# Fixed instruction orders, weight loads spread over the first segment, and a first K projection by halves, in a fused attention and gated-MLP kernel

## The chip, the cores and the metric

The kernel runs on one core of one Trainium2 chip. Times are device microseconds (us) of that core: medians over the executions listed with each result. One core has no second die to compare with, so a run counts as disturbed only if it is over 1.5% above the fastest of the same kernel. TensorE is called PE below, VectorE DVE, ScalarE ACT, GpSimd POOL and SyncE SP.

## The reference

Two branches read the same 2048 x 512 input and are mixed by a gate for each token. The attention branch has 32 heads of 16, four segments of 512 tokens, causal softmax inside a segment, and a linear memory carried from one segment to the next.

```python
for s in range(4):                                  # segments of 512 tokens
    logits = einsum('bhqd,bhkd->bhqk', qs, ks) * scale + mask   # causal
    p = softmax(logits); a_dot = einsum('bhqk,bhkd->bhqd', p, vs)
    num = einsum('bhld,bhde->bhle', phi(qs), M)     # memory of earlier segments
    den = einsum('bhld,bhd->bhl', phi(qs), z)[..., None] + 1e-06
    o = g * (num / den) + (1.0 - g) * a_dot         # g = sigmoid(beta), per head
    M = M + einsum('bhld,bhle->bhde', phi(ks), vs); z = z + phi(ks).sum(l)
a = concat(o) @ wo
b = (gelu(x @ w_gate) * (x @ w_up)) @ w_down        # 512 -> 1792 -> 512
gt = sigmoid((x * gate_w).sum(-1))
return gt * a + (1 - gt) * b
```

## The kernel before

The program is a graph of about a thousand tasks. A list scheduler runs while the kernel is built: it takes, over and over, the task that can start first by its own model of durations, with a priority (longest path plus a tuned bias for each kind of task) to break ties. The order in which it takes tasks becomes the fixed order of instructions on each engine. Each engine counts its finished instructions in one semaphore, so whoever waits for a task waits until the engine has passed that place in its list.

```python
while len(order) < n:
    for e in ENGINES:
        for t in ready[e]:
            st = max(cur[e], ready_at[t.id])
            ...                                   # exp first on ACT, patience for PV
            k = (st, -t.prio - (OPEN_BONUS if open_ else 0.0), t.id)
            if best is None or k < best[0]: best = (k, e, t)
```

The tasks that matter here, all for one segment s and a group t of eight heads: `qk` (row-tiled matmuls, 32 rows each, into one 2048-column PSUM tile), `exp` (ACT), `msk` (POOL zeroes what causality forbids), `pv` (column-tiled matmuls), `pvt` and `norm` (DVE). A task name such as `exp1_1B0` means segment 1, group 1, part B0; part L is the low rows. `G`, `U`, `D` are the gate, up and down matmuls, `K`, `Q`, `V` the projections, and a name with `ev` is the copy of its result out of PSUM. The masks and the loads before the change:

```python
# low rows: one select over 2048 columns
masks = [(PTl[:].rearrange("p g (b c) -> p (g b) c", c=64), [[0, 32], [2, 64]], 1, 2048)]
# other parts: one select of 256 columns for each key block
(bass.AP(PT[slot], c, [[2048, P], [512, 4], [1, 64]]), [[0, 4], [1, 64]], 64, 256) for c in offs
...
for a in range(4):
    dma(f"x0_{a}", (SP, ACT)[a % 2], ...)                     # x of segment 0
for c0, c1 in ((0, 128), (128, 512)):                         # columns 0-127, then the rest
    for key, w, src in (("wk", wk, A_wk), ("wq", wq, A_wq)):
        wdma((key, c0 > 0), SP, w[:, :, c0:c1], ...)
wdma("wv", ...); ...; wdma(("wg", 0), ...); wdma(("wg", 1), ...)
...
# after the first transposes of segment 0, in one lump on one queue
wdma(("wu", 0), ..., after=pk0); wdma(("wu", 1), ..., after=pk0)
wdma("wd", ..., after=pk0); wdma("wo", ..., after=pk0)
```

The softmax here doesn't subtract the row's maximum and nothing guards it: scores larger than these inputs give would overflow.

Of the kernel before, what the change touches and what calls it, by code (L numbers as in the profile page):

```python
# [13 lines left out]
ALU = mybir.AluOpType  # L14
# [18 lines left out]
PV_JOIN = 0.11  # L33
HOLD = 0.3
OPEN_BONUS = 6.0
BIAS = {
    "D0": -705, "D1": -805, "D2": -380, "D3": -442, "G0": -222, "G1": -900, "G2": -744, "G3": -86, "GdT0": 97,
    "GdT1": 844, "GdT2": -1, "GdT3": 895, "Gev0": 862, "Gev1": -349, "K0": 777, "K1": -529, "K2": 250,
    "K3": 307, "Q0": 715, "Q1": -519, "Q2": 584, "Q3": -641, "U0": -844, "U1": -888, "U2": -53, "U3": -206,
    "Um0": 900, "Um1": 148, "Um2": 49, "Um3": -86, "V0": 318, "V1": -357, "V3": 539, "Vev0": 540, "Vev1": 758,  # L40
    "Vev2": 262, "Vev3": -72, "Vlo0": -900, "Vlo1": 900, "Vlo2": -70, "Vlo3": 237, "consts": 21, "exp0": -666,
    "exp1": 177, "exp2": -517, "exp3": -395, "exsT0": 77, "exsT1": -899, "exsT2": -94, "exsT3": 695, "fin0": 37,
    "fin1": -471, "fin2": 741, "fin3": -517, "gbd": -146, "gelu0": -795, "gelu1": 416, "gelu2": 1, "gelu3": 126,
    "gexp": 402, "gexs0": -594, "gexs1": -701, "gexs3": 76, "gmat": -900, "gmul1": 900, "gmul2": -10,
    "gmul3": 319, "gsum0": -318, "gsum1": -86, "gsum2": -613, "gsum3": -900, "gts0": 73, "gts1": -850,
    "gts2": -487, "gts3": 848, "ident": 503, "kl0": -826, "kl1": -900, "kl2": -661, "kl3": 900, "kp0": 509,
    "kp1": 3, "kp2": -900, "kp3": -405, "masks": 769, "msk0": -290, "msk1": 789, "msk2": 116, "msk3": -63,
    "mz0": -162, "mz1": 638, "mz2": -319, "mzacc0": -423, "mzacc1": 170, "mzacc2": 439, "mzbd0": -25,
    "mzbd1": -178, "mzbd2": 70, "norm0": 704, "norm1": -880, "norm2": -46, "norm3": 166, "num2": -887,
    "num3": -200, "nump1": -900, "nump2": -220, "nump3": -164, "oTd1": 896, "oTd2": 268, "oTd3": 899,  # L50
    "omg": 528, "out0": 408, "out1": -644, "out10": 2, "out11": 869, "out12": 745, "out13": 461, "out14": -25,
    "out15": -280, "out2": 230, "out3": -27, "out4": 313, "out5": -134, "out6": 284, "out7": -18, "out8": 682,
    "out9": -139, "pkT0": 5, "pkT1": 569, "pkT2": 281, "pkc0": 489, "pkc1": -900, "pkc2": -14, "pke0": 310,
    "pke1": 399, "pke2": -73, "pqc1": 496, "pqc2": 14, "pqc3": -117, "pqe1": -17, "pqe2": 649, "pqe3": 63,
    "pv0": -95, "pv1": -551, "pv2": -900, "pv3": 30, "pvt0": -169, "pvt1": 86, "pvt2": -513, "pvt3": -26,
    "qk0": 417, "qk1": 185, "qk2": 503, "qk3": 669, "tload": 355, "vones": -877, "w": -765, "warm0": 21,
    "warm1": 747, "warm2": -324, "warm3": 371, "warm4": 223, "warm5": -120, "warm6": -334, "x0": -96,
    "x0ev0": 93, "x0ev1": 23, "x0t0": 596, "x0t1": 606, "x1": 367, "x2": -181, "x3": -900, "xt1": 533,
    "xt2": -189, "xt3": 11
# [42 lines left out]
class Task:  # L102


    def __init__(self, name, alts, grp=None, after=(), bias=0.0, nbytes=0):
        self.name = name
        self.alts = alts
        self.grp = grp
        self.after = tuple(after)
        self.bias = bias + BIAS.get(name[:re.search(r"[_.]|$", name).start()], 0.0)  # L110
        self.nbytes = nbytes
        self.tiled = None
        self.patience = 0.0
        self.ahead = False
        self.est = {e: sum(i.est for i in l) for e, l in alts.items()}
        rs, ws = set(), set()
        for l in alts.values():
            for i in l:
                rs.update(i.reads)
                ws.update(i.writes)  # L120
        self.reads, self.writes = rs, ws
        self.preds, self.succs = set(), set()
        self.prio = 0.0
        self.eng = None
        self.start = self.finish = None
        self.id = None


class Sched:
# [32 lines left out]
    def schedule(self):  # L162
        tasks = self.tasks
        n = len(tasks)
        groups = defaultdict(list)
        for t in tasks:
            if t.grp is not None:
                groups[t.grp].append(t)
        for g in groups.values():
            for t in g[1:]:  # L170
                for d in () if t.ahead or PE in t.alts else t.preds:
                    if d.grp is not g[0].grp and d not in g[0].preds:
                        g[0].preds.add(d)
                        d.succs.add(g[0])
        indeg = [len(t.preds) for t in tasks]
        topo = [t for t in tasks if indeg[t.id] == 0]
        for t in topo:
            for s in t.succs:
                indeg[s.id] -= 1
                if indeg[s.id] == 0:  # L180
                    topo.append(s)
        assert len(topo) == n, "cycle"
        for t in reversed(topo):
            best = max([s.prio for s in t.succs] + [0.0])
            t.prio = min(t.est.values()) + best + t.bias
        npred = [len(t.preds) for t in tasks]
        ready_at = [0.0] * n
        ready = {e: set() for e in ENGINES}
        for t in tasks:
            if npred[t.id] == 0:  # L190
                for e in t.alts:
                    ready[e].add(t)
        cur = {e: 0.8 for e in ENGINES}
        bank_free = {b: 0.0 for b in range(self.nbanks)}
        dma_free = 0.0
        order = []
        last_pe = None
        while len(order) < n:
            best = None
            due = min([ready_at[t.id] for t in ready[ACT] if t.tiled == "exp"] + [1e9])  # L200
            held = sum(t.tiled == "pv" and ready_at[t.id] <= cur[PE] + HOLD for t in ready[PE])
            for e in ENGINES:
                for t in ready[e]:
                    st = max(cur[e], ready_at[t.id])
                    if e == ACT and t.tiled != "exp" and st + t.est[e] > due + 0.1:
                        continue
                    if t.tiled == "pv":
                        if last_pe in ("qk", "pv") and ready_at[t.id] <= cur[e] and bank_free and \
                                min(bank_free.values()) <= cur[e]:
                            if best is None or (-1.0, 0.0, t.id) < best[0]:  # L210
                                best = ((-1.0, 0.0, t.id), e, t)
                            continue
                        st += t.patience
                    if t.grp is not None and t.grp.bank is None:
                        if len(bank_free) <= (0 if t.tiled == "pv" else held):
                            continue
                        st = max(st, min(bank_free.values()))
                    open_ = t.grp is not None and t.grp.bank is not None
                    k = (st, -t.prio - (OPEN_BONUS if open_ else 0.0), t.id)
                    if best is None or k < best[0]:  # L220
                        best = (k, e, t)
            assert best is not None, "deadlock in task graph"
            (st, _, _), e, t = best
            if t.tiled == "pv":
                st = max(cur[e], ready_at[t.id], min(bank_free.values()))
            for a in t.alts:
                ready[a].discard(t)
# [5 lines left out]
            if e == PE:  # L233
                if t.tiled == "pv" and last_pe == "pv":
                    t.finish -= PV_JOIN
                last_pe = t.tiled
# [14 lines left out]
            for s in t.succs:  # L251
# [3 lines left out]
                if npred[s.id] == 0:  # L255
                    for a in s.alts:
                        ready[a].add(s)
# [116 lines left out]
def _build(es, nc, A_x, A_wq, A_wk, A_wv, A_wo, A_beta, B_w_gate, B_w_up, B_w_down, gate_w, out):  # L374
# [108 lines left out]
    rank = [9000.0]  # L483
# [5 lines left out]
    def wdma(key, eng, dst, src, nbytes, nonc=False, after=()):  # L489
        rank[0] -= 20.0  # L490
        dma("w_" + str(key), eng, lambda: dst, lambda: src, [], [("w", key)], nbytes, bias=rank[0], nonc=nonc,
            after=after)

    def xdma(s, after=()):
        for kb in range(4):
            rank[0] -= 20.0
# [14 lines left out]
              [("c", "ident")], [("c", "ident")], 0.3)], bias=9990.0)  # L511
    task("tload", ACT, [Instr(lambda e: e.activation(stmp[:, 0:1], ones[:, 0:1], ACTF.Exp), writes=[("stmp",)],
                              est=1.5)], bias=8000.0)
    xin = hT[1][:, 0:4, :]
    for a in range(4):
        rank[0] -= 20.0
        dma(f"x0_{a}", (SP, ACT)[a % 2], lambda a=a: xin[:, a, :], lambda a=a: A_x[0, a * 128:(a + 1) * 128, :], [],
            [("hT", 1, a)], 131072, bias=rank[0], issue=0.45)
    for c0, c1 in ((0, 128), (128, 512)):
        for key, w, src in (("wk", wk, A_wk), ("wq", wq, A_wq)):  # L520
            wdma((key, c0 > 0), SP, w[:, :, c0:c1], r4(src)[:, :, c0:c1], 1024 * (c1 - c0) * (2 if c0 == 0 else 1))
    wdma("wv", SP, wv[:], r4(A_wv), 524288)
# [606 lines left out]
```

## Time and profile before

| | kernel before |
|---|---|
| time | 269.44 us, median of 3 (269.11 to 269.78) |
| span of the profiled run | 267.5 us |
| PE busy | 96%, full granted clock in every slice |
| chain of waits | 84% PE, 5% ACT, 1% POOL |
| first Q matmul / last matmul starts | 9.84 us / 264.58 us |

From the page of the kernel before: the span, the busy time of each engine, PE's granted clock in 40 slices (tenths), and the shares of the chain that ended last.

```profile
span 267.5 us, 7093 instructions
...
PE 257.9 (96%) x2965; PEld 118.4 (44%) x3005; DVE 199.9 (75%) x385; ACT 212.1 (79%) x188; POOL 102.3 (38%) x232
...
PEclk9999999999999999999999999999999999999999
...
PE 84%; ACT 5%; DVE 3%; issue 3%; DMA 2%; POOL 1%; SPq 0%; ACTq 0%; DVEq 0%
...
```

PE is the bound, and it has almost no room. A busy PE is not yet a PE at its peak, so I use the starts of consecutive matmuls in the trace and take off their columns at 2.4 per ns. Columns are 236.1 us of the span (the four tiles of a QK or PV group run side by side, so each counts for a quarter of its columns). What is left over is 27.8 us: about 3 ns for each plain matmul, 19 us of fixed gaps at 167 mode changes (whole array, row tiles, column tiles, with the memory update counted apart from PV: the gap is 0.11 or 0.15 us after QK, by the columns of its last matmul, 0.12 after PV, 0.10 after plain matmuls), 3.3 us in the head (the cold clock and the wait for wk), and about 1.8 us of real stalls, that is, of gaps beyond the usual one at their place. The Trainium skill, "TensorEngine Tiling (Array Packing)", Key Properties, says that changing the tiling mode drains TensorE; the gaps agree with it. "TensorE: Matmul & The Clock Gate", section "Wait — 56ns, not 53.3ns?", gives columns / 2.4 GHz plus about 2.5 ns for a warm matmul; this trace has 2.7 (median).

The table of waits of the kernel before: engine, line and tile, what was waited for: total us, times, longest.

```profile
...
POOL pt L814 <- ACT pt L810: 126.6, 55, 16.9
...
PEld psXALL L803 <- ACT pt L810: 22.5, 52, 0.7
...
POOL ptl L814 <- ACT ptl L810: 9.0, 5, 2.0
...
```

POOL waits for ACT's exps in 55 waits of 2.3 us on average: it follows them one by one, and for the low-row mask (`ptl`) it waits 9.0 us in all. PE's weight loads wait for exps, but that is hidden. The timeline of PE in the head of the kernel before (start us, duration us, engine, line, operation, tiles, count, idle before and releaser):

```profile
...
3.67 1.91 PE L540 MATMUL psXALL<-ident,hT 128*128 128x128 bf16 x16
5.45 1.50 PE L449 MATMUL psW<-xT,wk 128*128 128x256 bf16 x8
7.24 2.76 PE L449 MATMUL psW<-xT,wk 128*128 128x512 bf16 x12 [0.28 <-DMA wk<-in_A_wk_dram]
9.84 1.46 PE L449 MATMUL psW<-xT,wq 128*128 128x512 bf16 x6
```

All of x is transposed first, then K starts with the first 128 columns of wk, waits 0.28 us (0.45 between starts) for the others, and Q follows at 9.84 us.

### The profile page before, as it was taken

To read this page: it belongs to the slowest core of one execution; us is meant where nothing else is said; L and a number is where in the kernel's file an instruction comes from. 1 tells how busy PE (TensorE), PEld (TensorE's weight loads), DVE (VectorE), ACT (ScalarE), POOL (GpSimd) and SP (SyncE) were. 2 spreads that over 40 slices of the span, in tenths; PEclk is the share of its full clock that TensorE was granted. 3 is DMA by queue.
4 is the path that set the end of the run, shared out by engine and by line. 5 is a ranking of instruction groups with operands and counts; after the bars stand their busy time and mean duration, and the time that the engine had idled before them with its cause. 6 is when DMAs were issued, how large, how long until landed. Compare 5 with 4: busy or idle time off the path is not lost.

```text
span 267.5 us, 7093 instructions
## 1 busy us (share of the span) xinstructions
PE 257.9 (96%) x2965; PEld 118.4 (44%) x3005; DVE 199.9 (75%) x385; ACT 212.1 (79%) x188; POOL 102.3 (38%) x232
## 2 busy tenths in 40 slices
PE   8999999999999999999999999999999999999996
PEld 5444444344443443434354444444344444444354
DVE  1769799898989898889756877987952688753451
ACT  4889988899998997998858998887767767777602
POOL 8364553873002433485201433486300252352300
PEclk9999999999999999999999999999999999999999
DMA  6998992000203443000021224010020025001002
GB/s 192 228 328 184 390 241 42 1 2 0 44 0 79 81 101 102 22 20 2 0 44 39 42 59 124 21 44 2 0 44 0 2 59 42 0 22 36 8 0 78
DMA packets 33775, 18.22 MB, mean 68 GB/s; under 512 B 21456, under 2 KB 33744, under 8 KB 33744
## 3 DMA queue, kind: packets, MB, share of 16 engines
q1 hardware_dynamic: 33456, 17.51, 27.0%
q8 instruction: 23, 0.38, 0.6%
q10 hardware_dynamic: 288, 0.26, 0.3%
q14 instruction: 8, 0.07, 0.1%
HBM read 9.84 MB, written 2.10 MB: 45 GB/s over the span
## 4 chain that ended last, share of the span: by engine, by line
PE 84%; ACT 5%; DVE 3%; issue 3%; DMA 2%; POOL 1%; SPq 0%; ACTq 0%; DVEq 0%
PE psW L449 68%; PE psXALL L803 8%; PE psW L852 5%; ACT pt L810 3%; DMA wk<-in_A_wk_dram 2%; PE psXALL L449 1%; PE psW L860 1%; POOL exsT L712 1%; DVE tb L867 0%; PE psW L769 0%; ACT L937 0%; ACT L926 0%; SPq L480 0%; DVE mzbd L784 0%; DVE phkt L692 0%
## 5 line engine op out<-in xcount | busy, mean ns | idle before, releaser
L810 ACT ACTIVATE pt<-psXALL 128x2048 bf16<-128x2048 f32 x64 | 120.1, 1876 | 26.0 <-PE psXALL L803 23.9
L814 POOL TENSOR_SCALAR_AFFINE_SELECT pt<-pt 128x256 bf16<-128x256 bf16 x128 | 59.2, 464 | 131.6 <-ACT pt L810 126.6
L449 PE MATMUL psW<-xT,wu 128*128 128x512 bf16 x216 | 51.9, 380 | 0.8 <-issue 0.6
L449 PE MATMUL psW<-xT,wg 128*128 128x512 bf16 x214 | 50.2, 380 | 1.7 <-issue 1.3
L449 PE MATMUL psW<-wd,hT 128*128 128x512 bf16 x203 | 50.3, 380 | 0.9 <-issue 0.8
L958 DVE TENSOR_TENSOR hT<-psW,hT 128x512 bf16<-128x512 f32 x56 | 37.5, 684 | 11.4 <-PE psW L449 10.9
L449 PEld LDWEIGHTS psW<-xT,wg 128*128 128x128 bf16 x224 | 20.4, 98 | 25.7 <-issue 2.5
L449 PEld LDWEIGHTS psW<-xT,wu 128*128 128x128 bf16 x224 | 20.4, 98 | 24.5 <-issue 2.3
L867 DVE STREAM_TRANSPOSE tb<-psW 128x512 f32<-128x512 f32 x32 | 21.3, 697 | 12.6 <-PE psW L860 12.2
L449 PEld LDWEIGHTS psW<-wd,hT 128*128 128x128 bf16 x210 | 18.8, 98 | 22.5 <-issue 2.5
L803 PE MATMUL psXALL<-qT,kpad 32*128 32x320 bf16 (+3 forms) x512 | 25.8, 273 | 0.3 <-ACT pt L810 0.3
L937 ACT ACTIVATE hT<-psW 128x512 bf16<-128x512 f32 x28 | 15.9, 601 | 7.0 <-PE psW L449 6.9
L814 POOL TENSOR_SCALAR_AFFINE_SELECT ptl<-ptl 128x2048 bf16<-128x2048 bf16 x8 | 16.9, 2117 | 9.4 <-ACT ptl L810 9.0
L803 PEld LDWEIGHTS psXALL<-qT,kpad 32*128 32x128 bf16 x512 | 7.7, 92 | 27.6 <-ACT pt L810 19.6
L852 PE MATMUL psW<-pt,vaug 128*17 128x192 bf16 (+3 forms) x512 | 18.7, 273 | 0.0
L810 ACT ACTIVATE ptl<-psXALL 128x2048 bf16<-128x2048 f32 x8 | 15.0, 1876 | 3.6 <-PE psXALL L803 3.6
L449 PE MATMUL psW<-xT,wk 128*128 128x512 bf16 (+1 forms) x64 | 16.1, 376 | 0.8 <-issue 0.5
L712 POOL COPY exsT<-exs 32x4 f32<-32x4 f32 x64 | 15.4, 241 | 3.7
L466 DVE CAST hT<-psW 128x512 bf16<-128x512 f32 x21 | 14.1, 683 | 2.8 <-PE psW L449 2.5
L449 PE MATMUL psW<-wo,oT 128*128 128x512 bf16 x55 | 15.2, 380 | 0.5 <-issue 0.3
L449 PE MATMUL psW<-xT,wq 128*128 128x512 bf16 x60 | 14.9, 380 | 0.7 <-ACT qT L463 0.4
L449 PE MATMUL psW<-wv,xT 128*128 128x512 bf16 x62 | 15.0, 380 | 0.3 <-issue 0.3
(98 smaller groups left out, 300.0 us busy)
## 6 DMA issues: line engine op xcount, KB each, us to landing
out_dram<-ost SPq DMA_DIRECT2D x15, 128.0 KB, 1.7
wg<-in_B_w_gate_dram SPq DMA_DIRECT2D x2, 896.0 KB, 6.1
wu<-in_B_w_up_dram SPq DMA_DIRECT2D x2, 896.0 KB, 5.9
wd<-in_B_w_down_dram SPq DMA_DIRECT2D x1, 1792.0 KB, 12.1
phkt<-in_A_x_dram SPq DMA_DIRECT2D x3, 512.0 KB, 4.1
vlow<-vaug SPq DMA_DIRECT2D x8, 136.0 KB, 2.9
wv<-in_A_wv_dram SPq DMA_DIRECT2D x1, 512.0 KB, 6.2
wo<-in_A_wo_dram SPq DMA_DIRECT2D x1, 512.0 KB, 9.7
```

The source lines that it names most:

```text
L449: return Instr(lambda e: e.matmul(view(), lhsT, rhs, start=first, stop=last), reads=reads, writes=[fkey if fkey is not None else g.key], e ...
L466: alts[DVE] = [Instr(lambda e: e.tensor_copy(dst(), src()), reads=reads, writes=writes, est=dve_t(n))]
L712: cross = task(f"exsT{s}", POOL, [Instr(lambda e, g=g, c=c: e.tensor_copy(exsT[sl][32 * g:32 * g + 32, c:16:4], exs[32 * c:32 * c + 32, s4 ...
L803: instrs.append(Instr(lambda e, g=g, lhs=lhs, rhs=rhs, c0=c0, ncol=ncol: e.matmul(X[g][:, c0:c0 + ncol], lhs(32 * g), rhs(32 * g), start=T ...
L810: prev_exp[0] = exp_task(s, f"exp{s}_{t}{name}", [Instr(lambda e: e.activation(dst[:], XALL[:, :].rearrange("p (g c) -> p g c", g=4), ACTF ...
L814: task(f"msk{s}_{t}{name}", POOL, [Instr(lambda e, view=view, pat=pat, base=base: e.affine_select(out=view, in_=view, compare_op=ALU.is_ge ...
L852: instrs.append(Instr(lambda e, t=t, q=q, kb=kb, slot=slot, c0=c0: e.matmul(gp.f32()[32 * q:32 * q + 17, 128 * kb + 64:512], Vaug[sl][:, k ...
L860: instrs.append(Instr(lambda e, t=t, q=q, kb=kb, c0=c0: e.matmul(gp.f32()[32 * q:32 * q + 17, 128 * kb:128 * kb + 64], Vlow[j][:, kb, 4 * ...
L867: task(f"pvt{s}_{t}_{j}", DVE, [Instr(lambda e: e.transpose(Tb[:, j, :], gp.f32()[:, :]), [gp.key], [("Tb", j)], dve_t(512))], grp=gp)
L937: lambda e, g=g, ft=ft, s=s: e.activation(hT[s % 2][:, ft, :], g.f32()[:, :], ACTF.Gelu_apprx_tanh),
L958: task(f"Um{s}_{ft}", DVE, [Instr(lambda e, g=g, ft=ft: e.tensor_tensor(hT[sl][:, ft, :], g.f32()[:, :], hT[sl][:, ft, :], ALU.mult), [g.k ...
```

## The change

The scheduler no longer searches: every engine gets a list of task names and takes them in that order. The order is given as data (the lists are long and cut here); the model's durations were refined, among them a term for PE's mode switches, one for its cold start and one for blocks of 256 instructions. The low-row mask becomes four selects of 512. The first wk arrives as four groups of full rows ahead of the second half of x, and the first K projection runs by halves of the tokens and by weight rows. wu, wd (now in two halves) and wo wait for named exps of segment 0 instead of going out together. Also in the change, and not cut out below: wq and wv come by halves of their rows, the first Q projection goes to the PSUM tile of QK (`psXALL`), x of later segments is loaded at other places, and some copies move between ACT and DVE. The intent seems to be to fix an order found elsewhere, to keep PE fed at the start, and to keep big loads out of the way of small ones.

```diff
-BIAS = { "D0": -705, "D1": -805, ... }
+SWITCH = 0.097
+COLD = 5.8
+BLOCK, BLOCK_ASK, BLOCK_END = 256, 165, 208
+ORDER = {
+    "pe": ( "warm6 warm1 ... x0t0_0 x0t1_0 K0_2.0 K0_0.0 ... x0t0_1 x0t1_1 K0_2.2 ... Q0_0.0 ..." ),
+    "act": ( ... ),
+    "dve": ( "... mzbd0 gmul1 K1_3ev GdT0 Gev1_2 pvt0_0_1 ... mzbd2 Vev3_0 norm2_1 K3_2ev K3_0ev kp3_1 ..." ),
+    "pool": ( "... msk0_0B0 msk0_0L msk0_0A0 msk0_0B1 gbd msk0_0A1 omg exsT0 ..."
+              " msk1_0A1 msk1_1B1 msk1_1B0 msk1_1A1 msk1_1A0 msk1_2A0 ..." ),
+    "sp": ( ... ),
+}
 ... (schedule)
-                for t in ready[e]:
-                    ...
-                    k = (st, -t.prio - (OPEN_BONUS if open_ else 0.0), t.id)
+                t = queue[e][-1]
+                if npred[t.id]:
+                    continue
 ... (head)
-    for c0, c1 in ((0, 128), (128, 512)):
-        for key, w, src in (("wk", wk, A_wk), ("wq", wq, A_wq)):
-            wdma((key, c0 > 0), SP, w[:, :, c0:c1], r4(src)[:, :, c0:c1], ...)
+    x0dma(0)
+    x0dma(1)
+    for kb in range(4):
+        wdma(("wk", kb), (SP, ACT)[kb % 2], wk[:, kb, :], A_wk[128 * kb:128 * kb + 128, :], ...)
+    x0dma(2)
+    x0dma(3)
 ... (K projection)
-        nu = 2 if even is not None else 1
+        nu = 2 if head and wkey == "wk" else 1
 ... (low-row mask)
-                masks = [(PTl[:].rearrange("p g (b c) -> p (g b) c", c=64), [[0, 32], [2, 64]], 1, 2048)]
+                masks = [(PTl[:, g, :].rearrange("p (b c) -> p b c", c=64), [[0, 8], [2, 64]], 1, 512)
+                         for g in range(4)]
 ... (big weights)
-    wdma(("wu", 0), ..., after=pk0)
-    wdma(("wu", 1), ..., after=pk0)
-    wdma("wd", ..., after=pk0)
-    wdma("wo", ..., after=pk0)
+    for i, e in enumerate(("exp0_0B1", "exp0_1B0")):
+        wdma(("wu", i), ..., after=pk0 + [at[e]])
+    for i, e in enumerate(("exp0_2A0", "exp0_3A0")):
+        wdma(("wd", i), ..., after=[at[e]])
+    wdma("wo", ..., after=[at["exp0_3A1"]])
```

## The prediction

> **What bounds the kernel now.** TensorE, from the first weights to the end. The page gives PE 96% busy, full granted clock in every slice, and the chain of waits is 84% PE. A busy PE is not a PE at its peak, so I set the starts of consecutive matmuls in the trace against their columns. Between 7.24 us (K projection after its last wait) and the last matmul's start at 264.6 us nearly everything is accounted for:
> - about 233 us of columns at 2.4 per ns, plus about 3 ns per matmul, 3 us;
> - 167 changes between whole-array, row-tiled (QK) and column-tiled (PV) matmuls, each a fixed gap: 0.15 us after QK, 0.10 after plain matmuls, 0.13 after PV, about 21 us in all. The Trainium skill, "TensorEngine Tiling (Array Packing)", Key Properties, says that a mode change drains TensorE; these gaps agree;
> - other stalls: only about 0.6 us (0.3 at 100 us, 0.2 at 85 us).
>
> In the table of waits QK weight loads wait 22.5 us for exp, but the matmul gap stays 0.10 us: hidden. What remains is the head (7.2 us: x lands at 3.6, transposes, half-speed matmuls until 6.4, then 0.45 us waiting for wk) and the tail (2.6 us: one scaling, one output DMA).
>
> **What the change does.** Same matmuls and columns; order and DMA move.
> - Head: wk comes as full 1 KB rows on two queues ahead of the second half of x, and K runs by token halves, so PE starts after two x tiles. The 0.45 us wait should vanish; K may instead wait for the first PSUM copy (0.42 us). Estimate: gain 0.3 to 0.5 us. In the trace 256- and 768-byte packets move at 216 to 300 GB/s, larger ones at 380 to 400, so wq, wv and wg should still land before use.
> - Mode changes: the two programs' orders give 172 against 167, about +0.5 us. PV often stands beside QK now; PV-to-QK is not in the trace, and I assume 0.13 us.
> - Big weights spread over segment 0: PE did not wait for them before. Instruction fetches (23 of 16 KB, about 1 us each) cost a few tenths at most. Gain up to 0.3 us, with other stalls removed.
> - The low-row mask becomes four POOL selects instead of one of 2.1 us; POOL is 38% busy, hidden. So are moves between ACT and DVE.
> - Tail unchanged.
> - A new order brings small stalls of its own: +0.2 us.
>
> Sum: -0.4, +0.5, -0.3, +0.2, and a credit of 0.8 us because orders are usually kept only if they measured better. Predicted 268.6 us, 80% range 266.8 to 270.4. Faster by over 2%: 0.03; within 2%: 0.94; slower by over 2%: 0.03. With no stall and as many mode changes the floor is near 267 us, so order alone cannot give 2%.
>
> **What would show it.** Right: no wait for wk in the chain; K starts near 4.9 us; gaps at mode changes as before; span 266 to 268; stalls outside mode changes under 1 us. Wrong: a PE gap over 0.5 us naming wq, wg, xT or a copy to qT; exps of segment 0 delayed; PE stalls beside instruction fetches.
>
> **What would make it wrong.** PV-to-QK changes much cheaper or dearer than assumed (10 of them); x of segment 1, now issued later, landing after about 17 us; ACT late with the four qT copies before the first QK; the clock warming later.

## The result, and the profile after

| | before | after |
|---|---|---|
| time, median of 4 | 269.28 us (269.11 to 269.78) | 272.16 us (271.83 to 272.52) |
| span of the profiled run | 267.5 us | 270.5 us |
| first Q matmul starts | 9.84 us | 10.13 us |
| last matmul starts | 264.58 us | 267.65 us |
| left over beside the columns | 27.8 us | 30.8 us |

The ratio is 1.0104, 95% interval 1.0084 to 1.0125. Ratios here compare the fast runs of two kernels in the same rounds, so they are not quite the ratio of the medians that stand beside them.

The same lines of the page after the change:

```profile
span 270.5 us, 7141 instructions
...
PE 263.3 (97%) x3017; PEld 119.5 (44%) x3017; DVE 200.3 (74%) x388; ACT 211.9 (78%) x188; POOL 105.3 (39%) x256
...
PEclk9999999999999999999999999999999999999999
...
PE 82%; ACT 7%; POOL 6%; DMA 2%; issue 2%; DVE 1%; SPq 0%; ACTq 0%; POOLq 0%
...
```

PE's busy share rose to 97% while it lost 3 us: the share is useless for finding the loss (the trace of before also lacks 40 of its 3005 matmul records; the changed program has 3017, because halves make twelve more, of the same columns in all). The chain is a better hint: POOL's share of it went from 1% to 6%. The table of waits after:

```profile
...
POOL pt L875 <- ACT pt L871: 104.1, 24, 17.7
POOL ptl L875 <- ACT ptl L871: 36.5, 7, 14.4
...
PEld psXALL L864 <- ACT pt L871: 18.2, 41, 0.7
...
```

POOL's waits for the ordinary masks went from 55 (126.6 us) to 24 (104.1 us), and those for the low-row mask grew to 36.5 us with a longest of 14.4. POOL now waits seldom and long, then works off a pile. That it waits less in total for `pt` is no gain: it stands at the wrong mask.

PE's timeline in the head, after:

```profile
...
3.67 1.06 PE L596 MATMUL psXALL<-ident,hT 128*128 128x128 bf16 x8
4.83 0.94 PE L497 MATMUL psW<-xT,wk 128*128 128x256 bf16 x6
5.95 0.81 PE L497 MATMUL psW<-xT,wk 128*128 128x256 bf16 x6 [0.17 <-DMA wk<-in_A_wk_dram]
7.34 0.73 PE L596 MATMUL psXALL<-ident,hT 128*128 128x128 bf16 x8 [0.58 <-DMA hT<-in_A_x_dram]
7.92 2.38 PE L497 MATMUL psW<-xT,wk 128*128 128x256 bf16 x20
10.13 1.24 PE L497 MATMUL psXALL<-xT,wq 128*128 128x512 bf16 x5
```

K does start early (4.83 us), but the second half of x, now behind wk, landed only at about 7.3 us, and PE waited 0.58 us for it (0.75 between starts). Q begins 0.29 us later than before, not earlier.

After the head, the accounting of matmul starts gives the places where PE stood still. Neither kernel is without such places, but the ones below have no counterpart in the kernel before. First PE at 42 us, then DVE and POOL around it:

```profile
...
41.56 1.04 PE L497 MATMUL psW<-xT,wg 128*128 128x512 bf16 x4
43.00 1.25 PE L497 MATMUL psW<-xT,wg 128*128 128x512 bf16 x5 [0.41 <-DVE hT L514]
```
```profile
...
42.05 0.29 DVE L778 TENSOR_TENSOR gdT<-omgT,exsT 128x128 f32<-128x128 f32 x1 [1.45 <-POOL exsT L773]
42.26 0.68 DVE L514 CAST hT<-psW 128x512 bf16<-128x512 f32 x1
...
```
```profile
...
36.87 5.15 POOL L773 COPY exsT<-exs 32x4 f32<-32x4 f32 x16
42.15 4.36 POOL L875 TENSOR_SCALAR_AFFINE_SELECT pt<-pt 128x256 bf16<-128x256 bf16 x10
...
```

DVE's list has the tiny product `GdT0` (0.29 us) ahead of a copy out of PSUM that PE needs. `GdT0` waits for `exsT0`, sixteen copies on POOL, and POOL came to them late because its list begins with masks whose exps run later. PE pays 0.41 us of idle (0.58 between starts) for a product that is needed only later, by `norm0_0`.

At 113 us PE waits for masks themselves. PE, then POOL:

```profile
...
114.33 0.61 PE L914 MATMUL psW<-pt,vaug 128*17 128x448 bf16 x16 [0.27 <-POOL pt L875]
...
```
```profile
...
99.07 1.75 POOL L875 TENSOR_SCALAR_AFFINE_SELECT pt<-pt 128x256 bf16<-128x256 bf16 x4 [2.23 <-ACT pt L871]
110.03 5.94 POOL L875 TENSOR_SCALAR_AFFINE_SELECT pt<-pt 128x256 bf16<-128x256 bf16 x10 [9.22 <-ACT pt L871]
```

POOL stood idle for 9.22 us until 110.03, because `msk1_1B1` stands in its list ahead of `msk1_1B0`, `msk1_1A1` and `msk1_1A0`, while ACT makes the exps in the order A0, B0, A1, B1. Then it worked off ten selects in 5.94 us, and PV came before it was done. Last, 186 us:

```profile
...
187.51 1.25 PE L497 MATMUL psW<-wv,xT 128*128 128x512 bf16 x5 [0.82 <-DVE kT L514]
```
```profile
...
186.77 1.28 DVE L514 CAST kT<-psW 128x512 bf16<-128x512 f32 x2
```

PE stands 0.82 us because the PSUM bank for the V projection is freed by a DVE copy of K, which DVE's list places behind the chain of `norm2_1` and which starts at 186.77.

Added up, in starts of matmuls from the first Q on, each less the usual gap at its place: stalls grew from about 1.8 to about 4.0 us (after: 0.57 at 42, 0.31 at 52, 0.34 and 0.29 at 114, 0.89 at 186, 0.4 at 195 to 199, 1.2 in five waits for exps between 231 and 246), mode changes by 0.4, the head by 0.3. That is 2.9 of the 3.07 us. The five waits of the last segment have another cause than the masks, for they stay when the masks are sorted (below). In the intervals between QKs that end in them stand 1.7 to 1.9 us of columns, against 2.1 in most of the same intervals before, while one round of QK and exp takes 2.46 to 2.52 us there, which I read as PE running out of other work and waiting for the exp. No run changed that.

### The profile page after: what moved, and what is told of

Same layout as the page of the kernel before. It is cut to its first block, busy times and chain, and to the rows that moved or that the text cites. A ratio compares the mean times of both kernels' runs of the same rounds, so it can differ in the third digit from the quotient of the medians.

```text
span 270.5 us, 7141 instructions
## 1 busy us (share of the span) xinstructions
PE 263.3 (97%) x3017; PEld 119.5 (44%) x3017; DVE 200.3 (74%) x388; ACT 211.9 (78%) x188; POOL 105.3 (39%) x256
## 3 DMA queue, kind: packets, MB, share of 16 engines
HBM read 9.84 MB, written 2.10 MB: 44 GB/s over the span
## 4 chain that ended last, share of the span: by engine, by line
PE 82%; ACT 7%; POOL 6%; DMA 2%; issue 2%; DVE 1%; SPq 0%; ACTq 0%; POOLq 0%
PE psW L497 63%; PE psXALL L864 8%; ACT pt L871 6%; PE psW L914 5%; PE psXALL L497 3%; POOL pt L875 3%; DMA hT<-in_A_x_dram 2%; POOL exsT L773 2%; ACT ptl L871 1%; PE psW L922 1%; POOL gbd L645 1%; PE psW L830 0%; SPq L528 0%; PE psXALL L596 0%; POOL omgT L656 0%
## 5 line engine op out<-in xcount | busy, mean ns | idle before, releaser
L875 POOL TENSOR_SCALAR_AFFINE_SELECT pt<-pt 128x256 bf16<-128x256 bf16 x128 | 58.5, 467 | 108.9 <-ACT pt L871 104.1
L497 PE MATMUL psW<-xT,wu 128*128 128x512 bf16 x224 | 55.7, 380 | 0.0
L497 PE MATMUL psW<-wd,hT 128*128 128x512 bf16 x210 | 53.9, 380 | 0.0
L497 PE MATMUL psW<-xT,wg 128*128 128x512 bf16 x224 | 53.2, 380 | 0.4 <-DVE hT L514 0.4
L875 POOL TENSOR_SCALAR_AFFINE_SELECT ptl<-ptl 128x512 bf16<-128x512 bf16 x32 | 21.9, 685 | 38.1 <-ACT ptl L871 36.5
L497 PE MATMUL psW<-xT,wk 128*128 128x512 bf16 (+1 forms) x80 | 17.5, 340 | 0.3 <-DMA wk<-in_A_wk_dram 0.2
L497 PE MATMUL psW<-wv,xT 128*128 128x512 bf16 x64 | 16.3, 380 | 0.8 <-DVE kT L514 0.8
L497 PE MATMUL psW<-wo,oT 128*128 128x512 bf16 x60 | 16.3, 380 | 0.0
L773 POOL COPY exsT<-exs 32x4 f32<-32x4 f32 x64 | 14.5, 227 | 3.8
L914 PEld LDWEIGHTS psW<-pt,vaug 128*17 128x17 bf16 x512 | 10.2, 90 | 11.2 <-issue 4.2
```

The lines of the kernel that those rows point to most:

```text
L497: return Instr(lambda e: e.matmul(view(), lhsT, rhs, start=first, stop=last), reads=reads, writes=[fkey if fkey is not None else g.key], e ...
L773: cross = task(f"exsT{s}", POOL, [Instr(lambda e, g=g, c=c: e.tensor_copy(exsT[sl][32 * g:32 * g + 32, c:16:4], exs[32 * c:32 * c + 32, s4 ...
L875: task(f"msk{s}_{t}{name}", POOL, [Instr(lambda e, view=view, pat=pat, base=base: e.affine_select(out=view, in_=view, compare_op=ALU.is_ge ...
L914: instrs.append(Instr(lambda e, t=t, q=q, kb=kb, slot=slot, c0=c0: e.matmul(gp.f32()[32 * q:32 * q + 17, 128 * kb + 64:512], Vaug[sl][:, k ...
```

## The experiments

All outputs are right. Each gives the median, the ratio to the kernel before of the same rounds with its 95% interval, and that kernel's median where it matters (it lay between 269.0 and 269.6 throughout). By the record's 2% rule only the lump of weights is slower; the uncut mask is unclear and all others are the same, so what follows goes by the intervals and the traces.

### One product moved on DVE

```diff
 dve:  ... gmul1 K1_3ev
-      GdT0
       Gev1_2 pvt0_0_1 Gev0_13 gsum1_1 Gev1_12 gsum1_0
+      GdT0
       norm0_0 ...
```

> The changed kernel, with one item of the DVE list moved: the gate product GdT0, which waits for the POOL copies exsT, stands just before its only user, the first normalisation, and no longer ahead of three PSUM copies. Theory A (time is lost because an engine's fixed list puts an item that is not ready in front of items that TensorE needs): the 0.58 us PE gap near 42 us disappears and is not given back; time falls 0.4 to 0.6 us to about 271.6. Rival B (the loss is DMA: order of loads, big weights beside instruction fetches): the gap moves elsewhere, 272.0 to 272.3. Rival C (the loss is more mode changes): as B.

Measured: 272.02 us, ratio 1.0130 (1.0080 to 1.0179): no gain, where 0.4 to 0.6 us were expected (one of the four runs, at 274.68 us, widens the interval). The number is the one expected of the DMA rival; what speaks for the lists is the trace. The gap at 42 us was gone, and a larger one stood at 46 us. PE of this run:

```profile
...
46.60 0.61 PE L918 MATMUL psW<-pt,vaug 128*17 128x448 bf16 x16 [0.78 <-POOL pt L879]
...
```

PV waits 0.78 us for POOL's masks. Removing the wait that one sees first only let PE arrive earlier at the next thing that was late. Both are late on POOL, which the next run tests.

### POOL's masks in the order of the exps

Only the mask names in POOL's list are sorted by the order of their exps on ACT; other tasks keep their places.

```diff
-pool: msk0_0B0 msk0_0L msk0_0A0 msk0_0B1 gbd msk0_0A1 omg exsT0 msk0_1A1 ... msk1_1B1 msk1_1B0 msk1_1A1 msk1_1A0 ...
+pool: msk0_0A0 msk0_0B0 msk0_0L msk0_0A1 gbd msk0_0B1 omg exsT0 msk0_1A0 ... msk1_1A0 msk1_1B0 msk1_1A1 msk1_1B1 ...
```

> The changed kernel, with the masks of the POOL list sorted into the order in which the exps make them; the other POOL items keep their places. Theory A: the two PE gaps of 0.34 and 0.31 us before PV near 114 us go, and some smaller ones; time falls 0.5 to 0.8 us to about 271.5. Rivals B and C: within 0.3 us of 272.2.

Measured: 270.02 us, ratio 1.0037 (1.0010 to 1.0064). That is 2.1 us less than the changed kernel's 272.16, or 1.8 by the ratios, and more than the 0.5 to 0.8 expected. POOL in the same stretch as above, then PE:

```profile
...
102.75 1.04 POOL L879 TENSOR_SCALAR_AFFINE_SELECT pt<-pt 128x256 bf16<-128x256 bf16 x2 [1.81 <-ACT pt L875]
105.80 0.90 POOL L879 TENSOR_SCALAR_AFFINE_SELECT pt<-pt 128x256 bf16<-128x256 bf16 x2 [2.02 <-ACT pt L875]
108.39 1.99 POOL L879 TENSOR_SCALAR_AFFINE_SELECT pt<-pt 128x256 bf16<-128x256 bf16 x2 [1.69 <-ACT pt L875]
...
```
```profile
...
112.35 0.61 PE L918 MATMUL psW<-pt,vaug 128*17 128x448 bf16 x16
...
```

POOL's wait of 9.22 us is now several of about 2, one for each exp, and PV starts without a stall. The waits for the low-row mask fell from 36.5 to 12.5 us in all. The stalls at 42 and 52 us are gone too, though `GdT0` was not moved: `exsT0` starts at 35.33 instead of 36.87 us. From the first Q to the last matmul this run is 1.60 us shorter than the changed kernel; another 0.59 us comes from its head (Q at 9.54 us), which is scatter of the DMA and not of the edit, as shown below. So the order of POOL's list is worth about 1.6 us, the largest single cause. The stall that was at 186 us (now near 185) and the waits for exps in the last segment stayed.

### All three places mended

As above, with `GdT0` moved and the two K copies (`K3_2ev`, `K3_0ev`) ahead of `norm2_1` on DVE.

> The two edits above together, and a third: on DVE the copies of K3_2 and K3_0 out of PSUM stand before the normalisation norm2_1 and not behind it (the 0.85 us PE gap near 186 us). Theory A: the losses add, 0.58 + 0.65 + 0.7 us, so about 270.2 to 270.5, ratio to before near 1.003 to 1.005; what is left is the head (0.3) and the mode changes (0.5). Rivals B and C: 271.8 or more.

Measured: 271.56 us, ratio 1.0091 (1.0068 to 1.0114): worse than sorting alone, and a miss (270.2 to 270.5 expected). PE near 190 us:

```profile
...
190.38 0.61 PE L918 MATMUL psW<-pt,vaug 128*17 128x448 bf16 x16 [1.61 <-POOL pt L879]
...
```

The 0.89 us stall at 186 us was replaced by one of 1.46 us (between starts) at 188.39 us: DVE's copies of V, the first of which frees the PSUM bank that this PV is to use, now stand behind `norm2_1` and start only at 189.55. The profile names POOL, whose first select of this stretch ends at the same moment as PV starts; but, counted in the order of POOL's list, that select belongs to the next QK group (`msk2_3B0`), and the last mask that this PV needs had ended at 185.65. That the bank is what PV waits for is read from the order of the lists and not tested. The head was also an unlucky one (Q at 10.36 us). DVE is full in this stretch; its tasks can be exchanged, and the wait goes to whoever needs the one that was moved back.

### The order of before in the changed program

Every engine has the order of the kernel before, with its lump of weights; the new head loads, split K and cut mask stay.

```diff
-ORDER = the lists of the changed kernel
+ORDER = the lists that the scheduler of the kernel before makes (K0 by halves)
-    wdma(("wu", i), ..., after=pk0 + [at[e]])
+    wdma(("wu", i), ..., after=pk0)            # likewise wd, wo and x of segment 2
```

> The changed program (its DMAs at the start, K0 by token halves, four low-row masks, Q0 in the other PSUM tensor), but with the order of every engine written as the kernel before has it, big weights in one lump as before, K0 tiles in the order 0,1,2,3. Theory A: the order lists are the loss, so only the head's 0.3 us remains: 269.3 to 269.9. If the program's other parts (masks, head) cost: 270.5 or more. Rival C: 269.5 too, as it has 167 mode changes; told apart from A by e3.

Measured: 270.99 us, ratio 1.0065 (1.0044 to 1.0087). This missed: I had expected about the time of before. Its head was late (Q at 10.35 us), and the largest new stall is one of 1.36 us between two matmuls of the same PV group, for which the profile names no releaser:

```profile
...
100.54 0.24 PE L925 MATMUL psW<-ptl,vlow 128*17 128x64 bf16 x8
101.95 0.24 PE L925 MATMUL psW<-ptl,vlow 128*17 128x64 bf16 x8 [1.17 <-issue]
...
```

The kernel before has a small one (0.31 us between starts) at about the same time, but in a QK group, whose eight matmuls take 0.75 us in place of the usual 0.40:

```profile
...
100.34 0.75 PE L803 MATMUL psXALL<-qT,kpad 32*128 32x448 bf16 x8
...
```

In both, the gap stands ahead of matmul number 1107, counted from zero at the start of the program and with the missing records filled in, whatever matmul that is. This pointed to the position in the instruction stream, and gave the next experiment.

### The kernel before with twelve more warm-up matmuls

The seven warm-ups are cut into nineteen with the same number of columns; everything else is the kernel before.

```diff
-    for i in range(7):
-        n = 512 if i < 6 else 384
+    for i in range(19):
+        n = 192 if i < 17 else 96
```

> The kernel BEFORE, with its 7 warm-up matmuls cut into 19 smaller ones of the same 3456 columns in all (17 of 192, 2 of 96); every other instruction and order stays. This shifts every later TensorE instruction by 24 places against the 16 KB blocks in which instructions are fetched, to the 3017 matmuls of the changed kernel. Theory F (where a block border falls into the short PV matmuls, TensorE uses up the old block before the new one is there): a new gap of about 1.2 us inside the PV of segment 1 near 100 us, where the kernel before has gaps of 0.3 and 0.2, and time up by 0.7 to 1.5 us, ratio 1.003 to 1.006. Rival G (the 1.36 us gap of the run with the old order came from its data, the mask or a PSUM copy): ratio 1.000 within 0.001, no new gap.

Measured: 270.73 us, ratio 1.0054 (1.0033 to 1.0075), as expected. Its head was a good one (Q at 9.65 us), and most of the loss is here:

```profile
...
99.44 0.24 PE L860 MATMUL psW<-ptl,vlow 128*17 128x64 bf16 x8
100.76 0.24 PE L860 MATMUL psW<-ptl,vlow 128*17 128x64 bf16 x8 [1.07 <-issue]
...
```

Shifting the stream by twelve matmuls moved the gap from QK into PV, again to number 1107, and made it 1.26 us instead of 0.31. No data dependence changed. So PE has a costly place in its instruction stream. I take it for the border of a block of fetched instructions: the trace has 16 KB instruction fetches all along, one of them at 98.3 to 99.4 us here and one at 99.3 to 100.7 in the run before. In all five runs that show the gap, PE starts again 1.3 to 1.5 us after the end of such a fetch. The fifth is the kernel before with the mask cut, below: its PE stream is that of the kernel before, its fetch ended 0.2 us later, and its gap is 0.54 us in place of 0.31. A second gap of this kind stands at 164.5 us here (0.33 us) and at 165.7 in the run before (0.3 us), again 1.3 us after a fetch. That the fetch itself is what PE waits for is inferred from this, not shown. The Trainium skill, "Runtime: NRT & Kernel Launch", section "Instruction fetch mechanics", says that instructions are refilled in 16 KiB blocks of 256 and that crossing a border is "mostly hidden". These runs agree on "mostly": nearly all fetches leave no gap, this one costs up to 1.36 us among matmuls of 64 columns. The changed kernel comes to number 1107 some 4 us later, between matmuls of 448 and 320 columns and 5.5 us after the fetch (97.95 to 98.91), and has no gap there. Its planner has a term for such blocks, visible in the diff; whether it avoided the gap by that or by chance, no run tells.

### Big weights in a lump again

Only the loads of the changed kernel go back: wu and wd leave together ahead of `xt1`, the row-major copy of x for segment 1, and neither they, wo nor x of segment 2 wait for exps.

```diff
-sp: ... pkT0_1 xt1 w_wu0 x2_3 w_wu1 x2_2 x2_0 w_wd0 ... w_wo ... w_wd1 ...
+sp: ... pkT0_1 w_wu0 w_wu1 w_wd0 w_wd1 xt1 w_wo x2_3 x2_2 x2_0 ...
```

> The changed kernel, with one part undone: the two halves each of wu and wd are issued in one lump ahead of the second copy of x (xt1), and wo after it, as in the kernel before. Rival B (the spread loads collide with instruction fetches or with the x transposes and cost the time): 270.5 or less. Theory A (lists on POOL and DVE): the spread is neither the gain that was meant nor the loss, 271.8 to 272.5.

Measured: 278.28 us, ratio 1.0329 (1.0301 to 1.0356), slower, and far from both expectations. DVE, then PE:

```profile
...
44.59 1.23 DVE L757 TENSOR_TENSOR phkt<-phkt,gwb 128x2048 bf16<-128x2048 bf16 x1 [6.01 <-DMA phkt<-in_A_x_dram]
45.73 0.69 DVE L518 CAST kT<-psW 128x512 bf16<-128x512 f32 x1
...
```
```profile
...
41.51 0.40 PE L868 MATMUL psXALL<-qT,kpad 32*128 32x448 bf16 x8
46.48 4.45 PE L501 MATMUL psW<-xT,wg 128*128 128x512 bf16 x10 [4.57 <-DVE kT L518]
...
```

DVE's list has the gate product of segment 1 at this place, and its x is queued behind 3.7 MB: DVE waits 6.01 us, then PE 4.57 us for a copy. The matmuls after that start 0.427 us apart, which is half clock: the Trainium skill, "TensorE: Matmul & The Clock Gate", section "Wait — 56ns, not 53.3ns?", gives 426.7 ns for 512 columns on the cold array, and the trace agrees. The kernel before has the same lump and no such wait: there the lump left at 22.6 us, not 29.6, and x, issued at 28.4 in place of 33.7 us, landed at 37.3 and not at 44.6; its DVE comes to that product at 39.6 us, with x there. So the spread loads are no cause of the loss; with this order, in which the lump leaves 7 us later, they are needed.

### The head: x first, K over whole tokens

```diff
-sp: x0_0 w_wk0 w_wk2 x0_2 ...      act: x0_1 w_wk1 w_wk3 x0_3 ...
+sp: x0_0 x0_2 w_wk0 w_wk2 ...      act: x0_1 x0_3 w_wk1 w_wk3 ...
-        nu = 2 if head and wkey == "wk" else 1
+        nu = 1
```

> The changed kernel, with only the start altered: all four x tiles are loaded ahead of the wk rows, and K0 is projected over all 512 tokens by weight rows, kb after kb, and no longer by token halves. Theory A (the head lost because the second half of x was queued behind wk and landed at 7.3 us): Q0 starts at about 9.5 us and not at 10.1, the 0.75 us wait for x goes, time falls 0.4 to 0.8 us to about 271.5. If only the total of bytes counts: Q0 starts at 10.0 or later and nothing is gained.

Measured: 271.90 us, ratio 1.0092 (1.0077 to 1.0107). Q starts at 9.60 us, half a microsecond before the changed kernel's profiled run, and the median is only 0.26 us less, under the 0.4 to 0.8 expected. The seven profiled runs that share the changed kernel's head (it and six experiments) have Q between 9.42 and 10.36 us, mean 9.97, with nothing in the head different between them. The three with the loads of before have 9.65, 9.81 and 9.84. So the changed head is on average 0.1 to 0.2 us worse; no single profile can rank two heads this close.

The same head on the order of the kernel before:

> The changed program with the old order of every engine (as the run with the old order), but with the new start of x first and K0 over whole tokens, which also takes 16 matmuls away (3001 against 3017). Theories A and F: the head gains 0.3 us against the kernel before, the block border near 100 us moves out of the PV, so that gap falls to 0.5 us or less; 268.3 to 269.0, at or below the kernel before. If neither holds: 270.5 to 271.3 as with the old order alone.

Measured: 269.90 us, ratio 1.0025 (1.0007 to 1.0043): a miss. Q came at 9.50 us, and then the costly place in the stream took 1.06 us, again at number 1107, and a wait for an exp 0.8 us at 19 us. The gain of the head was spent twice over.

### The low-row mask uncut

In the changed kernel the mask is one select of 2048 again:

```diff
-masks = [(PTl[:, g, :].rearrange("p (b c) -> p b c", c=64), [[0, 8], [2, 64]], 1, 512) for g in range(4)]
+masks = [(PTl[:].rearrange("p g (b c) -> p (g b) c", c=64), [[0, 32], [2, 64]], 1, 2048)]
```

> The changed kernel, with one part undone: the low-row mask is again one POOL select of 2048 elements (2.1 us) instead of four of 512 (2.7 us or more together). Theory A says that POOL comes too late because of the order in its list, and here it has 0.6 us less to do for each pair of heads groups: the gaps near 42 and 114 us shrink but stay, 271.5 to 272.2. If the cut mask itself is the cause: gaps gone and 270.2 or less, as with the sorted list.

Measured: 273.45 us, ratio 1.0187 (1.0122 to 1.0251), a miss, and by the medians 1.3 us more than the changed kernel (one run of 276.55 us widens the interval; the other three lie between 273.1 and 273.6). DVE, POOL and PE near 50 us:

```profile
...
49.50 1.60 DVE L771 TENSOR_SCALAR stmp<-exs 128x4 f32<-128x4 f32 x1
...
```
```profile
...
48.95 2.12 POOL L879 TENSOR_SCALAR_AFFINE_SELECT ptl<-ptl 128x2048 bf16<-128x2048 bf16 x1 [1.86 <-ACT ptl L875]
```
```profile
...
52.00 0.35 PE L501 MATMUL psW<-mzbd,phq 128*128 128x136 bf16 x3 [0.57 <-DVE hT L518]
...
```

A DVE instruction on 4 columns, which takes 0.16 us elsewhere (median), takes 1.60 us and ends with POOL's select of 2.12 us. The Trainium skill, "SBUF — State Buffer", section "Who interferes with whom", says that DVE in some of its modes and GpSimd contend for a port pair that is locked for a whole instruction, so that the second to come blocks fully. The trace agrees, down to the common end. PE then waits 0.57 us for DVE's next copy. From the first Q to the last matmul this run is 1.45 us longer than the changed kernel; besides this wait, PE loses 0.7 us at 104 for a transposed copy of K that lands late, and 0.5 more than before at 188. DVE operations held by a select (1.0 us longer than their median at 93.0, 1.5 at 181.3) come before both, but that they are the cause was not traced. So cutting the mask was a real gain of the change. To see what it is worth elsewhere, the kernel before got the cut alone, with the order of every engine the same (on POOL, four selects in place of one):

> The kernel before with one edit: the low-row mask of 2048 columns becomes four selects of 512, every engine's order otherwise the same. Theory (the cut pays only where DVE is on TensorE's path; the kernel before has only about 0.6 us of stalls to give back): 269.0 to 269.5 us beside about 269.3, PE gaps unchanged within 0.2 us, while a small DVE operation that overlaps a low-row mask takes about 0.2 us instead of up to 2. Rival (the cut is worth the 1.3 us that undoing it cost in the changed kernel, in any order): 267.8 to 268.4 us.

Measured: 269.27 us against 269.44 of the same rounds, ratio 0.9985 (0.9953 to 1.0016): the same. The same DVE operation of 2048 columns, in the kernel before, then with the cut:

```profile
...
52.28 2.05 DVE L672 TENSOR_SCALAR kpad<-kT,maskc 128x2048 bf16<-128x2048 bf16 x1
...
```
```profile
...
52.32 0.75 DVE L672 TENSOR_SCALAR kpad<-kT,maskc 128x2048 bf16<-128x2048 bf16 x1
...
```

2.05 us became 0.75: DVE was held in the kernel before as well. The cut does not end the contention, it divides it: the two operations after this one became longer (0.78 to 1.07 and 0.94 to 1.18 us). PE gained nothing; in that order no wait of PE follows from it. On these two orders, then, the cut pays where DVE stands in PE's way.

### Two attempts at a version that beats both

The sorted masks, the new head, and DVE's copies for K and V ahead of `norm2_1`:

> The changed kernel with the POOL list in order of the exps, the new start, and on DVE the copies K3_2, K3_0, kp3_1, gsum3_1, Vev3_1 and Vev3_3 ahead of norm2_1 (the earlier third edit had left the V3 copies behind it, and TensorE then waited 1.46 us for their PSUM bank). Theory A: 0.5 us less for the head and 0.7 us less for the gap near 185 us than the POOL edit alone: 268.5 to 269.2, ratio 0.997 to 1.000. If orders only push waits about: 270 or more.

Measured: 271.13 us (270.65 to 272.78), ratio 1.0082 (1.0044 to 1.0120): a miss. wk landed late in the profiled run (PE waited 1.00 us, Q at 10.04 us), and 0.78 us was lost at 190.72 us, where the transposes out of PSUM behind `norm2_1` were now late.

The sorted masks, with the end of the down projection ahead of V on PE and on DVE one final copy (`fin1_3`) moved up and one sum (`gsum3_1`) moved behind two copies:

```diff
-pe: qk2_3A0 V3_1.0 V3_3.0 V3_3.2 V3_2.0 V3_1.2 qk2_3B0 D1_3.8 D1_3.10 pv2_2_1 ...
+pe: qk2_3A0 D1_3.8 D1_3.10 D1_3.12 D1_3.14 D1_3.16 qk2_3B0 V3_1.0 V3_1.2 V3_3.0 V3_3.2 pv2_2_1 ...
-dve: ... kp3_1 gsum3_1 Vev3_1 Vev3_3 ... pvt2_2_0 fin1_3 ...
+dve: ... kp3_1 fin1_3 Vev3_1 Vev3_3 gsum3_1 ... pvt2_2_0 ...
```

> The kernel with the sorted POOL list, with one more edit where DVE falls behind near 184 us: on TensorE the last ten matmuls of the output tile D1_3, which need no new PSUM bank, stand ahead of the QK that the V3 projection preceded, and V3 after it; on DVE the copies fin1_3, Vev3_1 and Vev3_3 stand ahead of a sum. Theory A (TensorE waits for a bank because DVE is behind there): the 0.9 us gap at 184 us goes and does not come back; 0.6 to 0.9 us below the sorted list alone, 269.1 to 269.5. If DVE is simply full there: the wait only moves, 269.8 to 270.3.

Measured: 270.75 us (269.56 to 270.91), ratio 1.0041 (1.0016 to 1.0067): a miss. The stall at 184 us was gone; 0.36 us stood at 192.5 and 0.64 at 196.8 instead. From Q to the last matmul it is 0.24 us better than sorting alone.

No version was faster than the kernel before.

## Why the prediction was wrong

The range (266.8 to 270.4) did not hold 272.16. Within 2% was right, the direction was not. Term by term, by matmul starts in the two traces:

| term of the sum | predicted | in the traces |
|---|---|---|
| head | -0.4 | +0.3 in this run, +0.1 to +0.2 over seven |
| mode changes, 167 to 172 | +0.5 | +0.4 |
| other stalls and fetches gone | -0.3 | about -1.8 |
| small stalls of the new order | +0.2 | about +4.0 |
| credit for a kept order | -0.8 | nothing |

The small stalls were misjudged by more than the total shows (3.8 us), because more of the old stalls went than was forecast (1.5 us); that part is luck.

**The step that failed** is the pair "A new order brings small stalls of its own: +0.2 us" and "a credit of 0.8 us because orders are usually kept only if they measured better". The new order's stalls are 4.0 us, and the 1.8 us that went with the old order do not make up for them. The largest part can be read off the lists: POOL's list takes masks in another order than ACT makes exps, and sorting it alone brought back 1.6 to 2.1 us. Of the rest, 1.2 us are waits for exps in the last segment, which no run touched, and 1.3 us stand between 186 and 199 us, where the runs mostly moved them. The credit was no reading of anything; it was a guess about how the order had come about, and nothing measured bears it out. The prediction's own list of what would show it wrong looked for gaps at weights, x and copies of Q; the large gaps after the head came at masks, at hT and at copies of K.

**Bound by PE, and no room for 2%: right.** All gains and losses are in tenths of a microsecond at PE's gaps, except where a load was made late on purpose.

**Mode changes: right.** PV to QK, which the trace of before did not have, came out at 0.12 us against 0.13 assumed, the same as PV to plain matmuls in the same trace.

**Head: mechanism half right, size wrong.** K did start near 4.9 us, and the wait for wk shrank from 0.28 us of idle to 0.17. What I left out is that wk was put ahead of the second half of x on the same queues: x landed at 7.3 us and PE waited for it instead.

**Big weights: right that PE did not wait for them before**; the runs add that this order cannot live without the spread (+6 us).

**"POOL is 38% busy, hidden": wrong.** POOL's share of busy time says nothing of when its results come. The order of POOL's tasks cost PE more than anything else, and making one POOL instruction long again cost 1.3 us, at least in part through DVE.

**Instruction fetches "a few tenths at most": true of the two kernels compared, wrong as a rule.** The order of before has 0.3 us there and the changed one none, but three other runs, in which the stream is shifted, lose 1.1 to 1.4 at the same place.

What stays open: about 0.2 us of the 3.07 not placed; whether other matmuls between the QKs of the last segment would end the 1.2 us of waits there; why x's landing scatters by about a microsecond between runs with the same loads; whether the gap at number 1107 is the fetch itself; and whether a better order exists in DVE's full stretch near 185 to 197 us, where three attempts only moved the wait.

## What to carry to other kernels

When an order is fixed as data, compare each consumer's list with the order in which its inputs are made: an in-order engine that stands at the wrong item makes everything behind it late, however idle it is on average. Read "hidden" from waits and their position, never from a busy share; and after mending one wait, look where the engine stops next before counting the gain. In a kernel this close to its bound, an edit that only shifts the instruction stream can cost a microsecond, as the twelve extra warm-ups did here, so test with a control that changes only the alignment.

## What the Trainium skill lacked or had wrong

- "Runtime: NRT & Kernel Launch", Instruction fetch mechanics: crossing a block is called "mostly hidden". Here one place in the stream costs PE 0.31, 0.54, 1.06, 1.26 or 1.36 us (five runs), at most 0.5% of the time, and PE starts again 1.3 to 1.5 us after a 16 KB fetch has ended; that it is a block's border is inferred.
- "TensorEngine Tiling (Array Packing)", Key Properties: names the drain at a mode change without a size. Here it is 0.10 us after plain matmuls, 0.11 or 0.15 after QK (row tiles) and 0.12 after PV (column tiles), together about 19 us of 267.
- "SBUF — State Buffer", Who interferes with whom: agrees. Sizes: an operation of 4 columns held for 1.60 us instead of 0.16, one of 2048 columns for 2.05 instead of 0.75 us.
- No page that I read gives the scatter of DMA landings from run to run: with the same loads the first Q matmul started anywhere from 9.42 to 10.36 us.
